# Pooled attention with a gated convolution feed-forward layer: batch 0 loaded as 32-bit words over another queue, some stores moved, last tiles at full height, a new order

## The chip, the cores and the metric

The kernel runs on one core of a Trainium2 chip. Its engines work side by side, each through its own fixed list of instructions: TensorE (PE, matrix products, with weight loads shown as PEld), VectorE (DVE), ScalarE (ACT), GpSimd (POOL) and SyncE (SP). SP and POOL also issue transfers (DMAs); these run on 16 DMA engines that all queues share. The metric is the device time of one execution in microseconds (us), the median of the runs shown; lower is better. A profile is one execution taken by the hardware profiler.

## The reference

There are 8 batches, 8 heads, 576 positions and a head dimension of 64. Keys and values are averaged over groups of 8 positions, which leaves 72 of each per head. The attention output, with the heads side by side (512 columns), goes through a feed-forward layer of 1,024 columns with a gate from a convolution over three positions.

```python
k_p = k.reshape(B, H, Sp, pool, D).mean(axis=3)          # pool = 8, Sp = 72
v_p = v.reshape(B, H, Sp, pool, D).mean(axis=3)
scores = scale * np.matmul(q, k_p.transpose(0, 1, 3, 2))
attn = softmax(scores)                                   # over the 72 pooled keys
x = np.matmul(attn, v_p)                                 # heads put side by side: (8, 576, 512)
h = np.maximum(x @ w_in, 0.0)                            # 512 -> 1024
conv_out[s] = sum over k of conv_w[k] * h[s + k - 1]     # three positions, zero outside
out = (h / (1.0 + np.exp(-conv_out))) @ w_out            # 1024 -> 512
```

Inputs and output are fp32. The products run in bf16 and accumulate in fp32.

## The kernel before

**Stages of a batch.** Each batch passes through the same steps, named as in the code.

- Loads. `load_k` and `load_v` fetch rows of 512 values, one row for each group of 8 positions (8 positions times 64); `load_q` fetches q with 8 consecutive positions on a partition, or, for batches 5 to 7, position by position. All of these, and the weights `w_in` and `w_out`, are issued by GpSimd, which casts fp32 to bf16 on the way. Beside them GpSimd has only a few memsets and masks. In its list a ninth transfer waits for the first of the eight before it.
- Pooling. `pool8` and `attn_k` add the 8 positions of k on DVE in three halving steps (L632, L639, L649). PE transposes the result (L662 for four full tiles of 128 rows, L663 for a last one of 64 rows) and `kz` copies it to a block layout (L669). `attn_v` does the same for v without the transposes, and multiplies by a mask that separates the heads (L700, L705). The mask is made on GpSimd.
- Queries. `regroup` brings the heads of q side by side (L453, on ACT or DVE, for batches 0 to 4). `attn_q` transposes q by PE (L735) and copies it out of PSUM (L744); for batches 5 to 7 it is transposed by DMAs on SP (L718).
- Scores. `attn_s` makes five tiles of products (L767; the fifth by narrow products, L769) and takes the exponential on ACT (L775).
- AV. `attn_av` makes five tiles of 128 positions, the last of 64, with four products (L792) and two more (L796) each. The sums of the weights come out of the same products; DVE takes their reciprocal (L805) and scales (L809) into `xx`. `xx` is transposed to `xT`, for batches 0 to 4 by PE (L829) and a copy (L835), for batches 5 to 7 by DMA transposes on SP (L822).
- Feed-forward. `mm1` (L849 in parts for batch 0, L872 after that) and its relu on ACT; `conv_off` on DVE and ACT (L918 to L945) or `conv_pe` on PE (L995) for a few columns; the gate, its product on DVE (L983); then `mm2` (L1026) for two batches at a time (a pair), a copy to `osb` (L1049, ACT or DVE, three buffers) and a store of up to 512 KB issued by SP (L1054). The last tile of all is done in two halves (L1039, L1044).

**What sets the order.** A planner in the program holds all operations with their dependencies, a written priority for each (`PARAMS["prio"]`) and estimates of their durations. It goes through them in modelled time, and the instructions are emitted in the order that it finds. Each engine then runs its list strictly in that order. `PARAMS["act"]` names the copies, scalings and the like that go to ACT rather than DVE. Where the planner sees a gap on PE in the first 60 us, `warm` fills it with products of a tile of zeros (L407).

**Lines that the change touches.** `load_k`, `load_v`, `load_q` and `regroup` for batch 0; the transposes in `attn_k`; the products in `attn_av` and the last `xx` transpose with its copy; the stores in `mm2`; the priorities and the ACT list. `gT`, two large buffers for the gated activations of a pair, are first written well after batch 0's attention.

Of the kernel before, what the change touches and what calls it, by code (L numbers as in the profile page):

```python
# [17 lines left out]
        "6 14 12 18 16 17 25 33 43 49 53 56 58 61 63 40 38 59 46 54 60 9 32 28 34 31 24 22 "  # L18
        "37 29 20 42 39 27 21 35 41 5 2 3 47 11 8 0 30 4 7 13 44 15 36 19 23 10 1 69 "
        "90 75 80 84 62 182 143 45 52 55 57 64 65 51 48 73 78 70 74 26 66 67 77 50 79 72 89 86 "  # L20
        "85 111 88 83 94 82 87 68 71 76 81 93 91 102 126 124 92 115 97 103 112 101 118 99 96 105 98 114 "
        "100 133 119 107 131 109 116 125 113 136 121 110 146 104 141 148 151 157 132 164 120 108 117 106 129 127 123 128 "
        "95 165 174 179 186 189 167 218 172 178 169 173 185 188 175 181 194 201 203 224 234 202 210 211 219 204 184 208 "
        "207 217 221 213 226 233 241 245 231 236 239 244 249 122 130 142 134 150 158 156 161 160 168 152 137 155 138 154 "
        "176 192 135 140 145 149 139 144 147 162 163 170 153 159 171 180 216 200 265 267 220 230 190 196 205 212 193 197 "
        "232 240 247 255 261 266 183 191 177 187 209 225 199 206 195 229 198 237 253 250 277 260 286 293 316 324 328 338 "
        "349 335 355 348 359 370 215 166 223 228 248 257 262 291 304 317 235 214 242 256 238 243 227 222 246 274 287 303 "
        "312 309 321 345 310 327 344 362 334 351 326 340 365 377 381 393 402 380 385 386 411 413 379 387 389 406 412 398 "
        "399 401 408 415 395 400 404 410 417 252 254 289 299 306 320 264 251 270 278 294 322 318 353 292 263 271 305 330 "
        "297 276 302 308 313 339 341 268 273 275 288 300 307 284 283 290 296 311 315 323 258 269 282 285 331 301 280 298 "  # L30
        "329 347 342 350 336 361 371 382 388 384 392 403 407 428 450 461 476 494 507 272 259 295 314 325 319 337 358 369 "
        "374 352 357 360 368 367 376 363 366 281 333 346 343 364 354 418 423 448 457 391 396 427 419 463 451 459 477 480 "
        "484 491 449 489 483 502 528 485 493 495 525 512 501 503 508 522 530 519 524 532 539 542 442 460 488 498 482 506 "
        "475 505 509 520 533 556 576 583 439 444 437 473 447 446 456 478 455 465 469 474 479 486 504 515 429 435 534 541 "
        "443 440 420 454 453 550 552 514 521 529 537 548 569 546 555 570 579 586 591 578 603 616 638 629 685 696 640 656 "
        "674 708 717 279 332 356 375 373 378 383 422 434 426 397 390 414 425 466 470 467 481 464 416 513 452 538 431 421 "
        "430 433 436 511 517 523 531 540 543 497 500 551 549 559 526 564 604 608 590 596 599 610 624 601 607 620 639 647 "
        "611 623 625 642 646 626 631 637 645 641 547 499 568 575 572 585 600 581 584 614 627 630 636 635 573 580 577 561 "
        "588 594 622 598 609 617 652 644 671 675 605 618 562 571 633 612 628 597 643 650 666 651 665 664 593 606 587 595 "
        "634 654 649 632 658 663 673 677 684 676 699 716 721 724 751 746 761 782 756 767 776 784 802 394 409 438 432 424 "  # L40
        "441 445 471 405 487 554 510 592 544 613 496 589 468 615 545 458 462 472 535 565 707 710 718 679 722 729 709 715 "
        "686 694 738 687 736 768 744 692 749 760 743 704 763 798 754 706 759 777 757 732 788 789 667 683 648 659 690 668 "
        "725 680 705 728 731 735 747 809 661 669 681 688 682 697 698 719 720 733 753 765 774 780 657 662 693 703 727 711 "
        "670 714 726 745 739 758 783 795 734 740 712 702 750 742 755 741 769 775 808 810 814 822 845 860 861 872 874 886 "
        "911 903 912 916 518 582 553 574 492 516 527 557 560 567 558 678 566 700 621 372 619 490 563 713 536 653 655 660 "
        "672 785 790 771 779 766 772 773 762 786 801 793 811 804 815 803 812 819 818 806 817 816 825 841 843 846 851 839 "
        "848 850 856 796 807 813 821 824 829 827 823 834 837 835 844 936 855 832 840 826 830 842 828 849 858 847 862 883 "
        "871 885 890 857 863 820 831 865 833 864 836 873 889 888 884 893 898 853 869 838 852 868 854 867 859 876 881 896 "
        "899 905 891 918 926 941 929 948 950 961 972 966 980 969 977 982 602 689 695 770 764 781 748 730 723 752 737 701 "
        "691 778 792 787 878 879 900 917 791 797 800 805 794 799 925 945 931 935 927 930 934 940 937 947 978 959 946 943 "  # L50
        "953 955 956 968 962 967 880 892 895 902 908 913 897 915 919 924 939 928 949 954 906 920 914 951 922 952 944 965 "
        "960 964 971 974 994 983 870 875 882 887 901 904 907 894 923 910 921 932 938 942 866 877 958 963 909 970 957 933 "
        "973 975 984 979 986 989 1010 1019 1014 1021 1025 1023 1032 1038 1041 1055 1005 1012 1000 1004 1008 1009 1015 1007 1020 1018 1024 1022 "
        "1028 1033 981 991 976 985 1027 1034 988 990 993 995 999 1037 1039 1002 1016 992 1001 1030 1035 1003 1011 1006 1013 1017 1045 1042 "
        "996 998 987 997 1046 1044 1026 1029 1031 1036 1040 1047 1048 1043 1051 1052 1059 1050 1053 1049 1056 1054 1058 1060 1071 1057 1061 1062 "
        "1064 1063 1066 1069 1067 1068 1065 1070 "
# [5 lines left out]
    "act": (  # L62
        "dw1.0 dw1.1 dw4.0 dw5.0 dw6.0 dw6.1 kz.0.0 qg.0.0 qTe.0.0 qTe.0.3 xte.0.2 kz.1.0 "
        "kz.1.1 qg.1.0 qTe.1.0 xte.1.0 xte.1.2 xte.1.4 cp0.0.0 oe.0.0 oe.0.1 oe.0.2 oe.0.3 kz.2.0 "
        "qTe.2.0 qTe.2.1 qTe.2.2 xte.2.0 xte.2.1 xte.2.2 cp2.1.0 cp2.1.4 oe.0.4 oe.0.5 oe.0.6 oe.0.7 "
        "oe.0.8 kz.3.0 qTe.3.0 xte.3.0 xte.3.1 xte.3.2 cp0.2.0 cp0.2.1 cp0.2.3 cp2.2.5 oe.1.0 oe.1.1 "
        "oe.1.2 oe.1.3 kz.4.1 qTe.4.2 xte.4.0 xte.4.1 xte.4.3 cp0.3.0 cp2.3.0 cp2.3.2 cp0.3.4 cp0.3.5 "
        "cp2.3.6 oe.1.5 oe.1.6 oe.1.7 oe.1.8 kz.5.0 kz.5.1 cp2.4.1 cp2.4.3 cp0.4.7 oe.2.2 cp0.5.2 "
# [32 lines left out]
    "qs": [1, 0, 0, 0, 0, 0, 0, 0],  # L101
    "xw": 0,
    "qd": [0, 0, 0, 0, 0, 0, 0, 0],
    "vp": [0, 0, 0, 0, 0, 0, 0, 0],
}


# [201 lines left out]
def kernel(  # L309
# [138 lines left out]
    def regroup(b, pr):  # L448
        if PARAMS["rg"][b] in "QT" or PARAMS["qd"][b]:
            return  # L450
# [707 lines left out]
```

## Time and profile before

| what | us |
|---|---|
| median of three runs | 201.82 (201.66 to 203.79) |
| the profiled run | 200.92 |
| its span, first to last instruction | 199.1 |
| PE busy | 190.8 |
| DVE busy | 171.0 |
| ACT busy | 167.0 |
| POOL busy | 47.5 |
| mm2 products (L1026, psfB) | 65.5 in 282 |
| mm1 products (L872) | 59.2 in 448 |
| products of zeros (L407, both tiles) | 14.9 in 206 |

The granted TensorE clock is 1.000 over the whole run. Busy time of PE counts from the start of a product to its modelled end, and neighbouring products overlap, so a busy PE may still lose time between two starts. In a row of the timeline the first number is the start in us from the beginning of the span, the second the duration; then come the engine, the line, the operation, the tile written and the tiles read, the shapes, and, in brackets, idle time before it and what ended it. "out<-in" names are the program's tiles; psfA, psbB and the like are PSUM tiles. L numbers are lines of the kernel above. In the table of stages each row begins with the stretch, its length, and the busy time of PE, PEld, DVE, ACT and POOL, with the number of instructions in brackets; the last three numbers are the granted clock, the share of the DMA engines and GB/s. Queue q0 carries GpSimd's transfers, q1 those that SP issues.

### The profile page before, as it was taken

The page shows a single profiled execution, that of the slowest core. Times are in us where ns is not written, and L with a number is a line of the kernel's source. Part 1 is how long each engine was busy: PE and PEld are TensorE (multiplying, and loading weights), DVE is VectorE, ACT ScalarE, POOL GpSimd, SP SyncE. Part 2 cuts the span into 40 slices and gives each one's busy share as a digit, 9 for nine tenths or more (in the row PEclk, how much of TensorE's full clock was granted, in tenths as well). Part 3 has the DMA queues.
Part 4 walks back from the last instruction along what each step waited for, and adds up shares of the span by engine and source line. Part 5 has one row for each costly group of instructions (what it writes and reads, how often), then busy time and mean ns, then how long its engine had stood idle before and what let it go on. Part 6 is the DMA issues. An engine that isn't in the chain of part 4 may idle for free.

```text
span 199.1 us, 4491 instructions
## 1 busy us (share of the span) xinstructions
PE 190.8 (96%) x1737; PEld 128.9 (65%) x1737; DVE 171.0 (86%) x400; ACT 167.0 (84%) x282; POOL 47.5 (24%) x76
## 2 busy tenths in 40 slices
PE   5999999999999999999999999989999999999992
PEld 5888777777546576767756656547666565765541
DVE  3777999999999999999999999988889997755631
ACT  0677699999995499999999999995999999998410
POOL 7966431543233262761140000000000000000000
PEclk9999999999999999999999999999999999999999
DMA  3999999999999999999999966477112144502324
GB/s 39 185 185 200 204 204 193 207 206 200 195 204 250 268 217 207 159 217 121 113 116 117 70 211 161 85 189 188 28 35 83 65 129 87 211 3 77 135 106 158
DMA packets 52857, 30.00 MB, mean 151 GB/s; under 512 B 33484, under 2 KB 48356, under 8 KB 52836
## 3 DMA queue, kind: packets, MB, share of 16 engines
q0 software_dynamic: 32912, 16.73, 68.1%
q1 hardware_dynamic: 19924, 12.99, 26.9%
q8 instruction: 13, 0.21, 0.4%
q14 instruction: 8, 0.07, 0.1%
HBM read 33.44 MB, written 9.44 MB: 215 GB/s over the span
## 4 chain that ended last, share of the span: by engine, by line
PE 88%; DVE 7%; POOL 2%; DMA 1%; issue 1%; ACT 0%; POOLq 0%
PE psfB L1026 31%; PE psfA L872 25%; PE psfA L792 4%; PE psfA L767 4%; PE psfA L995 4%; PE pswA L407 3%; PE psbB L735 2%; PE psfB L849 2%; DVE xx L809 2%; PE psfA L849 2%; PE psfA L796 2%; PE psbB L829 1%; PE pswB L407 1%; PE psbA L829 1%; DMA xT<-xx 1%; PE psfA L769 1%
## 5 line engine op out<-in xcount | busy, mean ns | idle before, releaser
L1026 PE MATMUL psfB<-w_out,gT 128*128 128x512 bf16 (+1 forms) x282 | 65.5, 378 | 0.0
L872 PE MATMUL psfA<-xT,w_in 128*128 128x288 bf16 x448 | 59.2, 286 | 0.9 <-DMA xT<-xx 0.7
L872 PEld LDWEIGHTS <-w_in 128*128 128x128 bf16 x448 | 42.8, 98 | 14.8 <-issue 1.2
L1026 PEld LDWEIGHTS <-gT 128*128 128x128 bf16 x290 | 27.2, 98 | 29.0 <-issue 0.2
L878 ACT ACTIVATE hT<-psfA 128x576 bf16<-128x576 f32 x56 | 35.2, 651 | 2.2 <-PE psfA L872 2.0
L918 ACT ACTIVATE cv<-hT,cr 128x576 bf16<-128x576 bf16 x37 | 28.3, 779 | 0.2
L809 DVE TENSOR_TENSOR xx<-psfA,rr 128x512 bf16<-128x512 f32 (+1 forms) x40 | 26.8, 683 | 0.9 <-DMA xT<-xx 0.7
L920 DVE TENSOR_SCALAR cv<-hT,cr 128x576 bf16<-128x576 bf16 x71 | 23.9, 363 | 3.9 <-ACT tg L945 2.3
L775 ACT ACTIVATE attnT<-psfA 128x576 bf16<-128x576 f32 x40 | 25.1, 674 | 0.3 <-PE psfA L767 0.2
L983 DVE TENSOR_TENSOR gT<-tg,hT 128x1152 bf16<-128x1152 bf16 x32 | 23.7, 750 | 1.2 <-ACT tg L1002 0.8
L927 DVE TENSOR_TENSOR cv<-cv,hT 128x1152 bf16<-128x1152 bf16 (+1 forms) x31 | 20.8, 672 | 4.0 <-ACT cv L918 3.9
L945 ACT ACTIVATE tg<-cv,cn 128x576 bf16<-128x576 bf16 x31 | 23.2, 775 | 0.9 <-DVE cv L937 0.6
L937 DVE TENSOR_TENSOR cv<-cv 128x1152 bf16<-128x1152 bf16 (+1 forms) x31 | 20.8, 673 | 0.2
L1049 ACT COPY osb<-psfB 128x512 f32<-128x512 f32 x24 | 14.3, 595 | 7.4 <-PE psfB L1026 7.3
L945 ACT ACTIVATE tg<-cv,cs 128x576 bf16<-128x576 bf16 x23 | 17.5, 797 | 0.0
L792 PE MATMUL psfA<-vblk,attnT 128*128 128x130 bf16 (+1 forms) x160 | 15.7, 222 | 0.2
L407 PEld LDWEIGHTS <-zero 128*128 128x128 bf16 x206 | 13.0, 105 | 3.4 <-DVE zero L520 2.5
L792 PEld LDWEIGHTS <-attnT 128*128 128x128 bf16 (+1 forms) x160 | 11.0, 100 | 4.1 <-issue 1.8
L407 PE MATMUL pswA<-zero 128*128 128x128 bf16 x148 | 10.5, 236 | 2.5 <-DVE zero L520 2.5
L767 PE MATMUL psfA<-qT,kz 128*128 128x512 bf16 x64 | 12.3, 286 | 0.4 <-ACT attnT L775 0.4
L439 POOL DMA_DIRECT2D q<-in_q_dram x10 | 8.6, 863 | 12.1 <-DMA k_b<-in_k_dram 4.0
L796 PE MATMUL psfA<-vblk,attnT 128*128 128x130 bf16 (+1 forms) x80 | 11.2, 221 | 0.0
(94 smaller groups left out, 247.8 us busy)
## 6 DMA issues: line engine op xcount, KB each, us to landing
out_dram<-osb SPq DMA_DIRECT2D x14, 512.0 KB, 3.0
k_b<-in_k_dram POOLq DMA_DIRECT2D x8, 512.0 KB, 14.8
v_b<-in_v_dram POOLq DMA_DIRECT2D x7, 512.0 KB, 16.7
q_b<-in_q_dram POOLq DMA_DIRECT2D x4, 576.0 KB, 17.6
out_dram<-osb SPq DMA_DIRECT2D x7, 256.0 KB, 2.1
w_in<-in_moe_w_in_dram POOLq DMA_DIRECT2D x2, 512.0 KB, 11.4
w_out<-in_moe_w_out_dram POOLq DMA_DIRECT2D x2, 512.0 KB, 15.0
q<-in_q_dram POOLq DMA_DIRECT2D x8, 128.0 KB, 12.6
```

Source lines behind the costliest of these rows:

```text
L407: nc.tensor.matmul(out=t, lhsT=zero[:, 0:P], rhs=zero[:, 0:P], start=True, stop=True)
L775: nc.scalar.activation(out=attnT[m][:, t, :], in_=slot(key).rearrange("p i x -> p (i x)")[:, 0:S], func=ACT.Exp, scale=1.0 / 64.0)
L792: nc.tensor.matmul(out=a[0:n, g, c * w:(c + 2) * w], lhsT=attnT[m][:, s, u0:u0 + n], rhs=vblk[m][:, 2 * s:2 * s + 2, :].rearrange("p x d - ...
L809: nc.vector.tensor_tensor(out=xx[i3][0:n].rearrange("p (g h e) -> p g h e", g=2, h=4), in0=av_view()[:, :, :, 0:D], in1=rr[i3][0:n].rearra ...
L872: nc.tensor.matmul(out=t[:, i, 0:HC], lhsT=w_in[:, c, f * P:(f + 1) * P], rhs=xT[m][:, c, i * HC:(i + 1) * HC], start=(c == 0), stop=(c == ...
L878: nc.scalar.activation(out=h_(b)[:, f, hs(b), 2:S + 2].rearrange("p (i x) -> p i x", i=2), in_=slot(key)[:, :, 0:HC], func=ACT.Relu)
L918: nc.scalar.activation(out=cv[y][:, kk // 2, z0:z1, :], in_=src, func=ACT.Copy, scale=sc)
L920: nc.vector.tensor_scalar(out=cv[y][:, kk // 2, z0:z1, :], in0=src, scalar1=sc, scalar2=None, op0=OP.mult)
L927: nc.vector.tensor_tensor(out=cv[y][:, 0, 0:n, :], in0=cv[y][:, 0, 0:n, :], in1=h_at(2), op=OP.add)
L945: nc.scalar.activation(out=tg[i3][:, zs[z0]:zs[z0] + z1 - z0, :], in_=cv[y][:, 0, z0:z1, :], func=ACT.Tanh if half else ACT.Sigmoid, scale ...
L983: nc.vector.tensor_tensor(out=o_, in0=tg[i3], in1=h2, op=OP.mult)
L1026: nc.tensor.matmul(out=a[:, 0, j0:j1], lhsT=g[:, c, t * P:(t + 1) * P], rhs=w_out[:, c, j0:j1], start=(c == 0), stop=(c == n_fb - 1), skip ...
```

## The change

- Batch 0's q, k and v are issued by SP instead of GpSimd. Nothing is cast: they land as fp32 words in the two `gT` buffers, which are idle then (`ks`, `ws`, `qs`). The first adds of k and v and the regroup of q read fp32. The regroup of batch 0 becomes four pieces of two heads, all on ACT. q comes first in SP's list (heads 4 to 7), then the convolution weights, k, the rest of q, and v.
- GpSimd's list therefore begins with memsets, the identity and then the loads of batch 1 and `w_in`.
- The stores of pairs 1 and 2 go to GpSimd's queue (ten stores), after all of its loads. Pairs 0 and 3 stay on SP.
- The last transpose of k takes 128 rows (64 of them zeros) instead of 64. The last tile of AV takes 128 columns of weights; the 64 beyond the end are the next tile's columns or a pad of zeros, and their results are not used. The last tile of `xx` goes through ordinary products with 128 rows into fp32 PSUM instead of 64-row transposes into bf16.
- Four memsets are added on DVE (the unwritten parts of the fp32 tiles, the two pads).
- The priorities and the ACT list are all new, and some estimates in the planner change, so that every engine's order differs. In the new lists PE has 146 products of zeros instead of 206. After batch 0, ACT has 5 scalings of the convolution fewer (32 of 108 instead of 37), 3 output copies more (27 instead of 24) and all five copies of `xx`'s last tiles; DVE the reverse.

```diff
@@ PARAMS
-    "prio": (...), "act": (...)
+    "prio": (...), "act": (...)
+    "kh": 2,
+    "sp": [0, 1, 1, 0],
...
-    perm4 = st("perm4", [64, 64], BF16)
+    perm4 = st("perm4", [P, 64], BF16)
...
-    attnT = [st(f"attnT{i}", [P, NT, S], BF16) for i in range(2)]
+    attnF = [st(f"attnT{i}", [P, NT * S + 64], BF16) for i in range(2)]
+    attnT = [a[:, 0:NT * S].rearrange("p (t s) -> p t s", t=NT) for a in attnF]
...
@@ load_q
+        if b == 0 and PARAMS["kh"] == 2:
+            for x in range(2):
+                for y, (r0, r1) in enumerate(((0, 64), (64, PR))):
+                    def fn(e, x=x, r0=r0, r1=r1):
+                        nc.sync.dma_start(out=qs[x][r0:r1].rearrange("p h i d -> p h (i d)"), in_=rows_q(b)[r0:r1, 4 * x:4 * x + 4])
...
@@ regroup
+        if b == 0 and PARAMS["kh"] == 2:
+            for h in range(0, H, 2):
+                def fn(e, h=h):
+                    copy_on(e)(out=q2[0][0:PR, :, h:h + 2, :], in_=qs[h // 4][0:PR, h % 4:h % 4 + 2].rearrange("p h i d -> p i h d"))
...
+    def early(i, lo, hi):
+        return gT[i].rearrange("p f s -> p (f s)")[:, lo:hi].bitcast(FP32)
+    ks = early(1, 0, NT * 1024).rearrange("p (t e) -> p t e", t=NT)
+    ws = early(0, 0, NT * 1024).rearrange("p (t e) -> p t e", t=NT)
+    qs = [early(i, NT * 1024, NT * 1024 + 4096).rearrange("p (h i d) -> p h i d", i=TP, d=D) for i in range(2)]
...
@@ load_k
+        if b == 0 and PARAMS["kh"]:
+            def fn(e):
+                nc.sync.dma_start(out=ks[:, 0:4], in_=src[0:512].rearrange("(t p) e -> p t e", p=P))
...
+                nc.sync.dma_start(out=ks[0:64, 4], in_=src[512:576])
...
@@ load_v
+        if b == 0 and PARAMS["kh"] == 2:
+            for c in range(4):
+                def fn(e, c=c):
+                    nc.sync.dma_start(out=ws[32 * c + 16:32 * c + 32, 4], in_=src[P:P + 16, c])
...
+            for x in range(2):
+                def fn(e, x=x):
+                    nc.sync.dma_start(out=ws[:, 2 * x:2 * x + 2], in_=src[0:P, 2 * x:2 * x + 2])
...
@@ attn_k
-            nc.tensor.transpose(out=t[:, 0, 512:576], in_=ksum[0:64, 4].rearrange("p i d -> p (i d)"), identity=ident[0:64, 0:64])
+            nc.tensor.transpose(out=t[:, 0, 512:640], in_=ksum[:, 4].rearrange("p i d -> p (i d)"), identity=ident)
...
@@ attn_av
-                nc.tensor.matmul(out=a[0:n, g, c * w:(c + 2) * w], lhsT=attnT[m][:, s, u0:u0 + n],
+                nc.tensor.matmul(out=a[:, g, c * w:(c + 2) * w], lhsT=attnF[m][:, s * S + u0:s * S + u0 + P],
...
-                nc.tensor.matmul(out=a[0:n, g, 0:4 * w].rearrange("p (c x d) -> p c x d", x=2, d=w)[:, :, 1], lhsT=attnT[m][:, 4, u0:u0 + n],
+                nc.tensor.matmul(out=a[:, g, 0:4 * w].rearrange("p (c x d) -> p c x d", x=2, d=w)[:, :, 1], lhsT=attnF[m][:, 4 * S + u0:4 * S + u0 + P],
...
-            a = slot(key2, True)
+            a = slot(key2, not last)
             for c in range(n_dc):
-                nc.tensor.transpose(out=a[:, 0, c * P:c * P + n], in_=xx[i3][0:n, c * P:(c + 1) * P], identity=(ident[0:n, 0:n] if tr else perm4 if last else perm))
+                if last:
+                    nc.tensor.matmul(out=a[:, 0, c * n:(c + 1) * n], lhsT=xx[i3][:, c * P:(c + 1) * P], rhs=ident[:, 0:n] if tr else perm4, start=c == 0, stop=c == n_dc - 1, skip_group_check=True)
+                    continue
+                nc.tensor.transpose(out=a[:, 0, c * P:c * P + n], in_=xx[i3][0:n, c * P:(c + 1) * P], identity=(ident if tr else perm))
...
@@ mm2
-            nc.sync.dma_start(out=out_rows[r:r + n * P, :].rearrange("(i p) d -> p i d", p=P), in_=osb[i3][:, 0:n, :])
+            (nc.gpsimd if PARAMS["sp"][pair] else nc.sync).dma_start(out=out_rows[r:r + n * P, :].rearrange("(i p) d -> p i d", p=P), in_=osb[i3][:, 0:n, :])
```

## The prediction

> **What bounds the kernel now.** I read the page's shares and its chain of waits first, then busy time by stage, then the timeline of the start, then the places where PE changes its tile, and last the DMA queues.
>
> ```profile
> PE 190.8 (96%) x1737; PEld 128.9 (65%) x1737; DVE 171.0 (86%) x400; ACT 167.0 (84%) x282; POOL 47.5 (24%) x76
> ...
> PE 88%; DVE 7%; POOL 2%; DMA 1%; issue 1%; ACT 0%; POOLq 0%
> ```
>
> PE carries 88% of the chain that ended last. The stages (columns: length, PE, PEld, DVE, ACT, POOL) show that it is not alone:
>
> ```profile
> 31.00:130.00 99.00, 98.80 (x895) 65.97 (x892) 97.18 (x225) 93.00 (x161) 28.10 (x36) 1.00 1.35 175
> 130.00:136.00 6.00, 4.65 (x52) 2.70 (x51) 5.07 (x14) 4.59 (x8) 0.00 (x0) 1.00 0.69 197
> ```
>
> From 31 to 130 us PE and DVE are both full (98.80 and 97.18 of 99 us), so time taken off PE alone is not all won. From 130 to 136 PE has a hole. The start is a chain of transfers (start, duration, engine, what):
>
> ```profile
> 8.45 0.82 DVE L632 TENSOR_TENSOR p<-k_b 128x1280 bf16<-128x1280 bf16 x1 [0.28 <-DMA k_b<-in_k_dram]
> 11.41 0.69 DVE L453 COPY q<-q_b 72x2048 bf16<-72x2048 bf16 x1 [0.33 <-DMA q_b<-in_q_dram]
> 14.79 0.56 DVE L632 TENSOR_TENSOR p<-v_b 128x768 bf16<-128x768 bf16 x1 [0.32 <-DMA v_b<-in_v_dram]
> 15.90 1.35 PE L407 MATMUL pswB<-zero 128*128 128x128 bf16 x21
> 17.09 0.40 PE L792 MATMUL psfA<-vblk,attnT 128*128 128x130 bf16 x4
> ```
>
> k is in at 8.45, q at 11.41, all of v at 14.79, and PE fills time with products of zeros until AV starts at 17.09.
>
> **Full tile height.** The first three rows are a last AV tile (64 columns of weights) and the product after it, the next two an ordinary AV tile, then k's transposes and what follows:
>
> ```profile
> 102.40 0.42 PE L792 MATMUL psfA<-vblk,attnT 128*64 128x130 bf16 x4
> 102.66 0.28 PE L796 MATMUL psfA<-vblk,attnT 128*64 128x130 bf16 x2
> 102.87 0.39 PE L1026 MATMUL psfB<-w_out,gT 128*128 128x512 bf16 x1
> ...
> 121.75 0.40 PE L792 MATMUL psfA<-vblk,attnT 128*128 128x130 bf16 x4
> 122.11 0.40 PE L792 MATMUL psfA<-vblk,attnT 128*128 128x130 bf16 x4
> ...
> 126.86 0.39 PE L662 MATMUL psbB<-ident,ksum 128*128 128x128 bf16 x4
> 127.31 0.66 PE L767 MATMUL psfA<-qT,kz 128*128 128x512 bf16 x4
> ```
>
> Starts count here, since ends overlap. A narrow AV tile holds PE from 102.40 to 102.87, 0.47 us; the product before it should have passed the array on at 102.31 (eight at 0.216 us from 100.58), so 0.09 more is lost going in. A full one holds it 0.36 (121.75 to 122.11). Gain 0.21 us; 7 of the 8 stand among real work (batch 0's does not): 1.5 us. k's five transposes hold it 0.45; at full height they are five like those of x, twelve of which take 0.67 in the chain, 0.056 each, 0.28. Gain 0.17 for batches 2 to 7 (0 and 1 are followed by zeros): 1.0 us. x's last tile (88.94 to 89.16, and 0.10 going in) costs 0.32; four products of 64 columns should pass like the 72-column ones of q (ten in 0.33 in the chain), 0.13. Gain 0.19 for batches 1 to 4: 0.8. Sum 3.3 us of PE.
>
> The Trainium skill, "TensorEngine Tiling (Array Packing)", section Theoretical Speedup, speaks against this edit: a dimension of at most 64 may run up to 2x faster in a small tile. By it the six narrow products would take half of 0.36 us, and making them full would cost 0.18 us seven times, 1.3 us, in place of the 1.5 won. The trace disagrees: four narrow products start 0.26 us after one another (102.40 to 102.66), four full ones 0.24 (121.75 to 121.99). That page's Key Properties say that a change of tiling mode drains the array, as the 0.09 us do.
>
> Will DVE and ACT let it through? Counted in the two orders, after batch 0, DVE gains 5 conv scalings (0.36 each) and a kz copy (0.31), loses 3 output copies (0.69), 4 x ends (0.28; all five go to ACT, now from fp32 PSUM) and 2 qT copies (0.53): -2.2 us. ACT loses 5 scalings (0.78) and a kz copy (0.39), gains 3 output copies (0.60), 4 x ends (0.39) and 2 qT copies (0.80): +0.8, with 6 us idle in the long stage. DVE's relief is below PE's 2.9 before 130 us; two narrow AV tiles (0.4) come later. I take -2.8; ends -0.4 (only those two) and -3.3.
>
> **Batch 0 as 32-bit words.** q, k and v are 576 rows of 2 KB each, 1,728 packets on SyncE's queue. A 512 KB store of 256 such packets shows the rate: alone 248 packets in 149.1 to 150.4 us, 190 a us; beside GpSimd's loads (60.1 to 62.1):
>
> ```profile
> q1 hardware_dynamic: 200, 0.41, 57.8%
> q0 software_dynamic: 266, 0.18, 55.8%
> ```
>
> 100 a us. A store issued at 56.33 behind a GpSimd backlog had its first packet at 60.04. SP issues from 0.81 us, 0.43 apart, first packets 1.0 us after issue (the cw_raw load): alone, k is in at about 7.5, q at 9.4, v at 12.5. But GpSimd, freed of batch 0, now starts batch 1's q at about 1.9 us; its first bulk ran 2.8 us after issue (k's, issued 2.16, full rate by 5.0). If that backlog waits behind SP's as the store did (3.7 us), the queues share from 8.4 and the last 680 packets need 7.1 us: v at 15.9. Reads on SP's queue beside loads are nowhere in this trace.
>
> What follows the data also grows. DVE's fp32 adds: by the 128x512 fp32 copies (0.69) 1.3 ns a column, so 0.95 and 0.65 us for v's pieces instead of 0.56 and 0.41, both now behind the last piece: 2.9 us to AV, against 2.3. ACT takes the whole q regroup, four of 0.95 (1.90 for 2048 columns); fp32 costs it nothing extra (fp32 and bf16 copies of 512 columns, 0.595 and 0.594). Its queue: conv weights in at about 5.0 (the load is now fourth on SP's queue), table 1.28, six scalings of 0.31, four regroups, one copy 0.63: 12.6. Then transposes 0.3, DVE copy 0.46, scores 0.4, five exps in 2.9: AV not before 16.7. So AV starts at 16.7 if SP's queue keeps ahead, 18.8 if it shares: -0.4 to +1.7 against 17.09. I take +0.8, leaning to the one row that shows a late comer waiting.
>
> GpSimd's early start pays in batch 1: 27 products of zeros (chain: 0.66, 0.78 and a bit) wait there around 27 to 30 us, after k at 24.5. Now k of batch 1 is in after 1,728 + 576 + 512 + 640 packets, at 190 a us about 21. I take -1.0 of 1.5; ends 0 and -1.5. Masks go behind eight loads on POOL (0.54 to 0.88 each), to about 9.5 us, hidden by the k add; if not, everything behind them on DVE waits. Four more memsets on DVE (the largest about 0.54, twice the 0.27 of 256 words) lie before any data.
>
> **Stores of pairs 1 and 2 on GpSimd's queue.**
>
> ```profile
> 130.64 0.53 SPq L1054 DMA_DIRECT2D out_dram<-osb  x1
> 131.26 2.68 SPq L822 DMA_TRANSPOSE xT<-xx  x2
> ```
>
> The transpose of x tile 3, batch 5, could follow the one that ended issuing at 130.55; it waits for the store's wait and issue to 131.26, tile 4 follows, and PE's products wait for them until 135.09. With only transposes queued, 0.7 us go directly, and more by the order. PE is idle 1.35 us in this stage and loses 3.0 by gaps between starts. I take -1.0; ends 0 and -3.0. On POOL the ten stores follow all loads (done at 108 us; the first such store ran at 114.19), so nothing queues behind them; three output buffers cover a slower landing, and without that cover one tile's 1.73 us waits.
>
> **New order.** Rewritten on every engine. PE loses about 4.5 us by gaps from 31 to 130 us; a different order can lose 2 more or less. I take 0.
>
> **Sum.** -2.8 + 0.8 - 1.0 - 1.0 = -4.0. Span 199.1 to 195.1, the profiled run 200.92 to 196.9; the median of the three runs is 0.9 higher (201.82), so 197.8.
>
> **Rivals.** (1) All comes through: SP's queue keeps its lead, DVE yields, the hole at 130 closes: -0.4 - 1.5 - 3.3 - 3.0 = -8.2, 193.6. For it: every piece has a row. Against: DVE's 98%.
> (2) Slower: GpSimd's loads interleave with batch 0 as soon as they flow, at 4.7 us. Some 440 packets are then through; the other 1,290 at 95 a us end at 18.3, AV starts at 21.6, 4.5 us late. DVE, which sets the pace to 130 us with its queue in fixed order, starts its full stretch that much later and eats the gain on PE but for 0.4: 201.8 + 4.5 - 0.4 - 1.0 = 204.9. It decides from a delay of 1.4 us on (over 1% from 3.4). For it: the equal shares at 60.1. Against: the 3.7 us before them. The Trainium skill, "DMA: Bandwidth & Descriptors", Rules for kernel authors, states it: spreading DMAs over issuing engines brings no bandwidth, they interleave. By that the time is this rival's; the shares agree.
> (3) Swallowed: SP nearly keeps up, but DVE holds PE and new gaps take the hole's place: +0.8 - 0.4 - 1.0 + 0.5 = -0.1, 201.7.
> That the edit is not made is excluded: the changed order has no narrow AV, k or x products and twelve batch-0 loads on SP.
>
> **Numbers.** Forecast 0.48 (195.8 to 199.8), rivals 0.22, 0.17, 0.13. About 1% is what a measurement here tells from no change: 199.8 to 203.8. Faster 0.22 + 0.46 = 0.68; same 0.13 + 0.02 = 0.15; slower 0.17. The range reaches from rival 1 to near rival 2: 193.6 to 203.6.
>
> **What would show it.** The first AV product near 17.9 us; v's add at 12.5 (SP ahead), 16 or 18.7 (interleaved); no zeros after the first AV tiles; AV's last tile 0.35 us long and k's transposes 0.28, with no 0.09 going in; fewer than 1 us of PE idle around batch 5's x; DVE below 98% in the long stage. Wrong if PE's idle or zeros grow by what the tiles save, or if DVE's adds of v start after 18 us.

## The result and the profile after

The changed kernel is slower: 210.45 us median of four runs (209.2 to 211.76) beside 202.12 (201.66 to 203.79) for the kernel before, measured beside it, a ratio of 1.0398 (95% interval 1.0307 to 1.0489). The forecast was 197.8, at most 203.6. The profiled run took 210.9 us with a span of 209.1. Ratios, here and below, leave out executions more than 1.5% above the fastest of the same kernel.

The first rows of the page, its row of the granted clock and the chain of waits answer to those of before:

```profile
PE 188.6 (90%) x1677; PEld 129.2 (62%) x1677; DVE 170.1 (81%) x400; ACT 169.1 (81%) x288; POOL 48.5 (23%) x76
...
PEclk9999997999999999999999999999999999999999
...
PE 52%; DVE 22%; DMA 11%; ACT 9%; issue 2%; SPq 1%; ACTq 0%; DVEq 0%
```

PE does 2.2 us less than before, yet carries only 52% of the chain instead of 88%; DMA, 1% before, has 11%. The place is the start. The timeline (start, duration, engine, line, what):

```profile
7.48 8.35 SPq L520 DMA_DIRECT2D gT<-in_v_dram  x3
...
8.31 0.30 PE L593 MATMUL psfB<-identf,cw_raw 24*128 24x24 f32 x1 [4.08 <-DMA cw_raw<-in_moe_conv_w_dram]
...
16.46 1.49 DVE L693 TENSOR_TENSOR p<-gT 128x1280 bf16<-128x1280 f32 x1 [3.12 <-DMA gT<-in_k_dram]
...
19.63 1.99 ACT L469 CAST q<-gT 72x1024 bf16<-72x1024 f32 x2 [4.35 <-DMA gT<-in_q_dram]
...
26.65 1.56 DVE L693 TENSOR_TENSOR p<-gT 128x768 bf16<-128x768 f32 x2 [3.97 <-DMA gT<-in_v_dram]
...
29.77 0.40 PE L861 MATMUL psfA<-vblk,attnT 128*128 128x130 bf16 x4 [3.67 <-DVE vblk L769]
```

The add of k starts at 16.46 us (8.45 before), that of v at 26.65 (14.79), each after a wait for its transfer, and AV at 29.77 instead of 17.09: 12.7 us late. The two transfers on the chain that ended last are k's, and the last of v's small pieces, which SP could issue only after it (start, duration):

```profile
2.98 12.53 DMA gT<-in_k_dram
15.53 10.91 DMA gT<-in_v_dram
```

The span is only 10.0 us longer, so what follows the first AV product is 2.7 us shorter, 179.3 instead of 182.0. The stages (columns as in the table of before):

```profile
31.00:130.00 99.00, 96.02 (x933) 67.72 (x931) 96.58 (x226) 91.44 (x163) 34.12 (x43) 0.98 1.24 168
130.00:136.00 6.00, 6.00 (x52) 3.89 (x50) 6.00 (x14) 5.98 (x11) 0.57 (x1) 1.00 0.50 114
```

The hole at 130 us is gone (PE 6.00 of 6.00 instead of 4.65). DVE is below 98% from 31 to 130, but PE is now idle for 3 us there.

The edits on PE came out as read. k's transposes, an AV tile and the last tile of x, each with the product behind it:

```profile
62.79 0.39 PE L727 MATMUL psbB<-ident,ksum 128*128 128x128 bf16 x4
63.01 0.22 PE L728 MATMUL psbB<-ident,ksum 128*128 128x128 bf16 x1
63.07 2.40 PE L1067 MATMUL psfA<-hT,dw 128*128 128x288 bf16 x18
...
83.45 0.40 PE L861 MATMUL psfA<-vblk,attnT 128*128 128x130 bf16 x4
83.69 0.28 PE L865 MATMUL psfA<-vblk,attnT 128*128 128x130 bf16 x2
83.81 1.89 PE L1098 MATMUL psfB<-w_out,gT 128*128 128x512 bf16 x8
85.53 0.28 PE L899 MATMUL psfB<-perm,xx 128*128 128x64 bf16 x4
85.65 0.61 PE L901 MATMUL psbA<-perm,xx 128*128 128x128 bf16 x8
```

By starts: 0.28 us for k, 0.36 for an AV tile, 0.12 for x, with no narrow tile and no 0.09 us of change left.

What the queues did shows in the packets from 9 to 13 us (queue, packets, MB, share of the 16 engines):

```profile
q0 software_dynamic: 384, 0.38, 56.3%
q1 hardware_dynamic: 379, 0.76, 55.7%
```

Batch 0 on q1 and batch 1 with `w_in` on q0 take turns here, 95 packets a us each. Before that it was no equal share: from 6 to 8 us GpSimd's queue had 457 packets through and SP's 90.

### The profile page after: what moved, and what is told of

It is laid out like the page before. It is cut to its first block, busy times and chain, and to the rows that moved or that the text cites. A ratio compares the mean times of both kernels' runs of the same rounds, so it can differ in the third digit from the quotient of the medians.

```text
span 209.1 us, 4391 instructions
## 1 busy us (share of the span) xinstructions
PE 188.6 (90%) x1677; PEld 129.2 (62%) x1677; DVE 170.1 (81%) x400; ACT 169.1 (81%) x288; POOL 48.5 (23%) x76
## 4 chain that ended last, share of the span: by engine, by line
PE 52%; DVE 22%; DMA 11%; ACT 9%; issue 2%; SPq 1%; ACTq 0%; DVEq 0%
PE psfB L1098 21%; PE psfA L944 19%; DMA gT<-in_k_dram 6%; DMA gT<-in_v_dram 5%; DVE p L693 4%; PE psfA L861 3%; DVE cv L992 3%; DVE xx L878 2%; DVE cv L1009 2%; DVE p L701 2%; DVE cv L999 2%; PE psfA L1098 2%; ACT tg L1017 2%; ACT hT L928 1%; PE psfA L1067 1%
## 5 line engine op out<-in xcount | busy, mean ns | idle before, releaser
L1098 PE MATMUL psfB<-w_out,gT 128*128 128x512 bf16 (+1 forms) x274 | 63.5, 377 | 0.1
L992 DVE TENSOR_SCALAR cv<-hT,cr 128x576 bf16<-128x576 bf16 x76 | 26.5, 372 | 2.3 <-ACT hT L928 0.9
L1017 ACT ACTIVATE tg<-cv,cn 128x576 bf16<-128x576 bf16 x32 | 24.6, 792 | 1.5 <-DVE cv L1009 1.5
L990 ACT ACTIVATE cv<-hT,cr 128x576 bf16<-128x576 bf16 x32 | 24.8, 793 | 0.2
L1121 ACT COPY osb<-psfB 128x512 f32<-128x512 f32 x26 | 15.1, 596 | 8.2 <-PE psfB L1098 7.9
L1126 POOL DMA_DIRECT2D out_dram<-osb x10 | 6.9, 686 | 63.4 <-ACT osb L1121 39.7
L861 PE MATMUL psfA<-vblk,attnT 128*128 128x130 bf16 x160 | 15.8, 223 | 4.2 <-DVE vblk L769 3.7
L861 PEld LDWEIGHTS <-attnT 128*128 128x128 bf16 x160 | 11.8, 100 | 8.3 <-issue 4.2
L415 PEld LDWEIGHTS <-zero 128*128 128x128 bf16 x146 | 11.8, 123 | 4.0 <-DVE zero L568 3.5
L447 POOL DMA_DIRECT2D q<-in_q_dram x10 | 9.5, 949 | 9.0 <-DMA v_b<-in_v_dram 4.4
```

Source lines behind the costliest of these rows:

```text
L861: nc.tensor.matmul(out=a[:, g, c * w:(c + 2) * w], lhsT=attnF[m][:, s * S + u0:s * S + u0 + P], rhs=vblk[m][:, 2 * s:2 * s + 2, :].rearran ...
L990: nc.scalar.activation(out=cv[y][:, kk // 2, z0:z1, :], in_=src, func=ACT.Copy, scale=sc)
L992: nc.vector.tensor_scalar(out=cv[y][:, kk // 2, z0:z1, :], in0=src, scalar1=sc, scalar2=None, op0=OP.mult)
L1017: nc.scalar.activation(out=tg[i3][:, zs[z0]:zs[z0] + z1 - z0, :], in_=cv[y][:, 0, z0:z1, :], func=ACT.Tanh if half else ACT.Sigmoid, scale ...
L1098: nc.tensor.matmul(out=a[:, 0, j0:j1], lhsT=g[:, c, t * P:(t + 1) * P], rhs=w_out[:, c, j0:j1], start=(c == 0), stop=(c == n_fb - 1), skip ...
```

## The experiments

All times are beside runs of the kernel before on the same chip. The table gives, from the profiled execution of each, the start of the first AV product, the span, and what lies between that product and the end, which is nearly the same work in every kernel (the height of the tiles differs, and how much of batches 0 and 1 falls ahead of it). It is one execution each, and that of before, 200.92 us, is faster than its median, so differences of a microsecond in these columns prove little. The last column is the ratio of the times, over all runs, with its interval.

| kernel | first AV | span | after it | ratio |
|---|---|---|---|---|
| before | 17.09 | 199.1 | 182.0 | 1 |
| changed | 29.77 | 209.1 | 179.3 | 1.0398 (1.0307 to 1.0489) |
| e1 before, full height | 18.11 | 199.9 | 181.8 | 0.9937 (0.99 to 0.9974) |
| e4 before, stores moved | 17.94 | 200.4 | 182.5 | 1.0034 (0.9994 to 1.0073) |
| e2 changed, GpSimd held for v | 20.57 | 205.1 | 184.5 | 1.0174 (1.0099 to 1.025) |
| e3 changed, GpSimd held for k | 21.74 | 200.3 | 178.6 | 1.0006 (0.9965 to 1.0046) |
| e7 e3, k in halves | 23.86 | 204.7 | 180.8 | one run, 206.52 us |
| e8 changed, loads back on GpSimd | 24.03 | 203.5 | 179.5 | 1.0112 (1.0077 to 1.0148) |
| e9 e8, k on SP | 23.92 | 202.5 | 178.6 | 1.0105 (1.0073 to 1.0138) |
| e10 changed, only q on SP | 20.72 | 199.2 | 178.5 | 0.9983 (0.994 to 1.0026) |
| e11 e8, regroup divided | 19.81 | 198.7 | 178.9 | 0.9938 (0.9906 to 0.9969) |
| e12 start in order of arrival | 21.50 | 199.6 | 178.1 | 0.9957 (0.9928 to 0.9985) |
| e13 e12 with narrow tiles | 21.01 | 201.5 | 180.5 | 1.0046 (1.0012 to 1.0081) |
| e14 scores in pairs | 20.13 | 198.5 | 178.4 | 0.9942 (0.9912 to 0.9973) |
| e15 e14 without zeros between | | | | 0.9922 (0.9889 to 0.9955) |

**Full height alone, in the old order.**

```diff
# before.py; likewise k's last transpose and the last tile of xx
-    out=a[0:n, g, c * w:(c + 2) * w], lhsT=attnT[m][:, s, u0:u0 + n],
+    out=a[:, g, c * w:(c + 2) * w], lhsT=attnF[m][:, s * S + u0:s * S + u0 + P],
```

> The kernel before with the full-height ends of k, AV and x alone, in its old order. Theory (PE sets the pace, DVE lets most through): last AV tile 0.36 us on PE instead of 0.47 and no 0.09 going in, k's transposes 0.28 instead of 0.45; 2.0 to 3.3 us less, about 199.3. Rival (DVE, 98% busy from 31 to 130 us, holds PE): less than 0.7 us, about 201.6, with new gaps on PE where the tiles shrank.

It gained 0.63%, 1.3 us (0.5 to 2.0), between the two. The profiled execution doesn't show this gain (its span is 0.8 us longer, with a start 1.0 us later), but its stages say where time stayed; the row from 60 to 100 us is from e1, with that of before under it:

```profile
31.00:130.00 99.00, 96.93 (x895) 65.82 (x888) 96.42 (x224) 91.82 (x160) 29.90 (x37) 1.00 1.39 176
130.00:136.00 6.00, 4.76 (x52) 2.60 (x50) 5.26 (x14) 5.79 (x11) 0.00 (x0) 1.00 0.64 164
```

```profile
60.00:100.00 40.00, 39.42 (x416) 28.62 (x415) 39.81 (x95) 34.81 (x61) 16.60 (x20) 1.00 1.50 194
60.00:100.00 40.00, 39.83 (x412) 28.11 (x409) 39.16 (x95) 34.47 (x61) 16.13 (x21) 1.00 1.51 193
```

For the same 895 products from 31 to 130 us PE is busy 1.87 us less than before (98.80), but the stretch holds no more of them: the time became idle time on PE. Up to 100 us DVE is full (39.81 of 40 us), so it holds the pace there. After that DVE itself waits for a load; the first add of one batch's k, in e1 and in before:

```profile
113.29 0.83 DVE L634 TENSOR_TENSOR p<-k_b 128x1280 bf16<-128x1280 bf16 x1 [2.19 <-DMA k_b<-in_k_dram]
111.78 0.82 DVE L632 TENSOR_TENSOR p<-k_b 128x1280 bf16<-128x1280 bf16 x1 [0.32 <-DMA k_b<-in_k_dram]
```

So a second thing stood behind PE here, the arrival of k on GpSimd's queue, which the prediction has nowhere among its limits of this stage. How much of the gain it kept back is not known; it is one execution.

**Stores of pairs 1 and 2 alone, in the old order.**

```diff
# before.py
-            nc.sync.dma_start(out=out_rows[r:r + n * P, :]...
+            (nc.gpsimd if pair in (1, 2) else nc.sync).dma_start(out=out_rows[r:r + n * P, :]...
```

> The kernel before with the stores of pairs 1 and 2 on GpSimd's queue alone, old order. Theory (the transposes of batch 5's x wait behind a store on SP): the transposes that were issued at 131.26 go out 0.5 to 0.8 us earlier, the product after them starts at about 134 instead of 135.1, total 0.7 to 1 us less, about 201.2. Rival (the hole comes from the order, xx itself is late): within 0.3 us of before, 202.

No gain: the interval runs from 0.12 us less to 1.5 more, and the rival's "within 0.3 us" lies in it. The hole stays (PE busy 4.38 of 6 us, 4.65 before):

```profile
130.00:136.00 6.00, 4.38 (x50) 2.56 (x49) 4.51 (x12) 5.02 (x9) 0.72 (x1) 1.00 0.81 189
```

So the store between two transposes on SP did not make it. In the changed kernel it went with the new order, stores moved; tall tiles are not needed for that (e13, with narrow ones, has PE busy 5.95 of the 6 us), and the order without the moved stores wasn't tried.

**GpSimd's loads held back.** A small copy on GpSimd, ahead of its first load, reads what SP loads, so that load waits; the masks are moved ahead of it.

```diff
# after.py
+            if o.name == "ldq1.0":                     # GpSimd's first load
+                nc.gpsimd.tensor_copy(out=held, in_=ws[:, 0:4, 0:1])   # e2: v's two large pieces
+                nc.gpsimd.tensor_copy(out=held, in_=ks[:, 0:4, 0:1])   # e3 instead: k's large piece
```

> The changed kernel, but GpSimd's first load (batch 1's q) follows a small copy that reads both large pieces of batch 0's v, so that no GpSimd load runs beside batch 0; the masks come before it. Theory (the loads of GpSimd halve SP's queue): k's first add at 8 to 10 us instead of 16.5, v's at 13 to 15 instead of 26.7, first AV product at 17 to 18.5 instead of 29.8, and the total 8 to 11 us under 210.4, less what batch 1 and w_in then come late. Rival (SP's queue reads fp32 slowly by itself): v's add after 18 us, AV after 21.

> The same, but GpSimd's loads wait only for k's large piece. Theory: k's add at 8 to 10 us as in the run that holds for v; the 832 packets behind it share from there on: v's add at 17 to 19, first AV product at 20 to 22, and the total between that run and the changed kernel, or below both if batch 1's loads matter more. Rival (SP slow by itself): k's add at 12 or later.

With v awaited (e2), v's add starts at 17.23 and AV at 20.57: 9.2 us of the 12.7 are gone, so GpSimd's loads beside batch 0's cost that much. AV lies between the 17 to 18.5 of the theory and the "after 21" of its rival. But batch 1's q then comes too late: PE waits 2.9 us for its copy and runs at half clock from 24 to 31 us, and the rest is 184.5. With k awaited (e3) GpSimd's packets begin at 15 us, and the time is that of before (1.0006): AV is still 4.65 us late, and 3.4 us come back behind it. k was in at 10.9 us, where the expectation had 7.5:

```profile
12.04 1.48 DVE L694 TENSOR_TENSOR p<-gT 128x1280 bf16<-128x1280 f32 x1
...
18.63 1.56 DVE L694 TENSOR_TENSOR p<-gT 128x768 bf16<-128x768 f32 x2 [1.25 <-DMA gT<-in_v_dram]
...
21.74 0.40 PE L862 MATMUL psfA<-vblk,attnT 128*128 128x130 bf16 x4 [0.95 <-DVE vblk L770]
```

Still, even with SP's queue alone, v's large pieces (in at 16.4 us, when GpSimd's held copy ran in e2) are far from the 12.5 of the forecast. In e3 the queue carries k between 7 and 9 us, q's second piece between 9.8 and 12 (packets, MB, rate of the stretch):

```profile
DMA packets 376, 0.76 MB, mean 382 GB/s; under 512 B 3, under 2 KB 3, under 8 KB 376
```

```profile
DMA packets 219, 0.44 MB, mean 198 GB/s; under 512 B 6, under 2 KB 6, under 8 KB 219
```

q goes at half of k's rate. q's pieces fill 64 partitions, k's 128.

**k cut into two pieces of 64 partitions**, on e3.

```diff
# e3
-                nc.sync.dma_start(out=ks[:, 0:4], in_=...
+                for p0 in (0, 64):
+                    nc.sync.dma_start(out=ks[p0:p0 + 64, 0:4], in_=...[p0:p0 + 64])
```

> The kernel that holds GpSimd's loads until k's large piece is in, with that piece (128 partitions) cut in two of 64 partitions each, one behind the other on SyncE's queue. There q's two pieces of 64 partitions went at 198 GB/s (9.8 to 12 us), k's of 128 at 382 (7 to 9 us). Theory (the number of partitions sets it): k's pieces go at about 200 GB/s, k's add comes at 14 to 15 instead of 12.04 us, v's at 21 instead of 18.63, first AV near 24, span near 203. Rival (it is how q lies in memory, or the first touch of a tensor): k's pieces at 350 to 390 GB/s, add at 12 to 12.5, AV at 21 to 22.5, span 199.5 to 201.5.

From 7 to 9 us, where k went at 382 GB/s:

```profile
DMA packets 210, 0.40 MB, mean 199 GB/s; under 512 B 16, under 2 KB 16, under 8 KB 210
```

The same words from the same rows of memory now go at half the rate, v's add moves from 18.63 to 20.75 us and AV to 23.86, as expected; k's own add came earlier than the 14 to 15 expected, at 12.90. It is one run. Rows, words and queue are the same, so it is the number of partitions. The Trainium skill, "SBUF — State Buffer", section "Door 1: The DMA port swizzle (why `[64,N]` ≈ `[32,N]`)", states it: partitions 0 to 63 reach only 8 of the 16 ports, with 196 GB/s measured for 64 partitions and 328 for 128. These runs agree on 64 partitions, with 198 and 199, and on the halving; their 382 for 128 is above the page's 328.

**Batch 0 back on GpSimd's queue, all else as changed.** In e5 and e6 batch 2's load of q stood ahead of half of batch 0's regroup, which therefore waited for it and read batch 2's q for four heads: the two kernels (e5 with all on GpSimd, 1.1071, 1.1007 to 1.1136; e6 with k on SP, 1.0963, 1.0896 to 1.103) say nothing on the question.

> The changed kernel with batch 0's q, k and v back on GpSimd's queue as bf16, issued before batch 1's; every engine's other work in the changed kernel's order, stores and full tile height kept. Theory (the loss is all in batch 0's loads; behind the first AV product the changed kernel was 2.7 us shorter, 179.3 instead of 182.0 us, by the tiles and the order): first AV between 17 and 18.5 us as before, span near 197, time 198 to 199.5, ratio 0.975 to 0.987. Rival A (the shorter body came from batch 1's loads, which ran while PE waited for batch 0): AV at 17 to 18.5, products of zeros back around 25 to 30 us, body 181 to 182, span 199 to 200, ratio 0.99 to 1.00. Rival B (the new order itself costs): ratio over 1.01.

> As the run before, but k of batch 0 on SyncE's queue as 32-bit words, with nothing but the convolution weights ahead of it; q and v on GpSimd's queue. Theory (two queues share one rate of some 180 packets a us, so it matters only that what shares with batch 0 is batch 0 itself; the second queue starts earlier): k's add at 9 to 11 us, q's regroup at 9.5 to 11, v's add at 13.5 to 14.5, first AV at 16 to 17.5, 0.5 to 1.5 us before that of the run with all on GpSimd's queue, time as much less. Rival (sharing delays k and q each to the end of both): k's add at 11.5 or later, first AV at 18 or later, time 0.5 to 1.5 us more than that run's.

With that load behind the regroup (e8, e9):

```diff
# after.py; e9 leaves k's load as it is and moves DVE's adds of k ahead of its first copy of transposed q
-                nc.sync.dma_start(out=ks[:, 0:4], in_=...
+                nc.gpsimd.dma_start(out=k_b[0][:, 0:4], in_=...        # v and q likewise
+        plan.insert(plan.index(by["qg.0.0"]) + 1, by["ldq2.0"])
```

> Batch 0's q, k and v on GpSimd's queue again, the rest as in the changed kernel, with batch 2's load of q now behind all four pieces of batch 0's regroup (in the first attempt it stood ahead of two of them). Theory (the loss is all in batch 0's loads; behind the first AV product the changed kernel is 2.7 us shorter, 179.3 instead of 182.0 us, by the tiles and the order): first AV between 17 and 18.5 us, span near 197, time 198 to 199.5, ratio 0.975 to 0.987. Rival A (the shorter body came from batch 1's loads, which ran while PE waited for batch 0): AV at 17 to 18.5, zeros back around 25 to 30 us, span 199 to 200, ratio 0.99 to 1.00. Rival B (the new order itself costs): ratio over 1.01.

> As the run before, but k of batch 0 on SyncE's queue as 32-bit words behind the convolution weights, and DVE's adds of k ahead of its first copy of transposed q. In the first attempt k's packets went at 157 to 189 a us from 3 to 5 us and were through by 7.3, q's by about 9.5. Theory: k's add at 8 to 8.5 us, q's regroup at 10.5 to 11, v's add at 13.5 to 14.2, first AV at 16 to 17, 0.5 to 1.5 us ahead of the run with all on GpSimd's queue, time as much less. Rival (something else ends last before AV, ACT's four pieces of the regroup and the exponentials behind them): AV within 0.4 us of that run's, same time.

Both missed the start that was expected, with AV at 24 us, and are 1.1% slower than before. (e8's ratio is its rival B's, over 1.01, but the loss lies ahead of AV and not behind it.) The timeline of e8:

```profile
11.14 1.99 ACT L470 COPY q<-q_b 72x1024 bf16<-72x1024 bf16 x2 [1.71 <-DMA q_b<-in_q_dram]
...
14.47 4.53 PE L415 MATMUL pswA<-zero 128*128 128x128 bf16 x54
...
15.23 1.99 ACT L470 COPY q<-q_b 72x1024 bf16<-72x1024 bf16 x2
...
20.69 0.88 DVE L694 TENSOR_TENSOR p<-v_b 128x768 bf16<-128x768 bf16 x2
```

Data is not late here: nothing in the last three rows waits for a transfer. The four pieces of the regroup are all on ACT, the second pair behind scalings and a copy, and 54 products of zeros, set for a q that comes early, hold PE until 19 us. So the new order has a start that was laid out for other arrival times. In e9 k's add came at 8.80 us, near the 8 to 8.5 expected, and nothing came of it, as the rival had it: v's add at 20.57, AV at 23.92. But behind AV both have 178.6 to 179.5 us, like the changed kernel.

**Only q on SP.**

```diff
# after.py: q as changed, k and v on GpSimd ahead of batch 1; in the order:
+        for n in ("qT.0.1", "av.0.0"):
+            pl.gaps[by[n][3].i] = (0.6, *pl.gaps[by[n][3].i][1:])    # shorter blocks of zeros
```

> The changed kernel with q of batch 0 on SyncE's queue as now, but its k and v on GpSimd's queue as bf16, ahead of batch 1's loads; two blocks of products of zeros ahead of the first AV product cut to 0.6 us each. Theory (what hurts is batch 1's loads beside batch 0's, and q's pieces of 64 partitions passing at half the rate of k's; with q alone on one queue its slowness is covered by k and v on the other, and what follows the first AV product takes 178.6 to 179.5 us as in the runs with the changed order): q's first regroup at 7 to 8 us, k's add at 9 to 10, v's add at 13 to 14.5, first AV at 16 to 17.5, span 195 to 197, time 197 to 199, ratio 0.973 to 0.985. Rival A (start as good, but what follows grows by what the start saves, since batch 1's loads come later): span 199 to 200, ratio 0.99 to 1.00. Rival B (two queues start each other late, v's add after 16): AV after 18.5, ratio above 0.99.

A miss at the start, as its rival B had it: q's regroup began at 12.03 us, not 7 to 8, k's add at 13.96, not 9 to 10, v's at 18.28 and AV at 20.72. From 4 to 12 us q on SP and k on GpSimd took turns (187 packets to 217 from 6 to 8). The time is that of before.

**The start mended, loads on GpSimd.**

```diff
# e8
+        block = [(x, "DVE", z, o) if o.name in ("qg.0.6", "qg.0.4") else (x, y, z, o) ...]   # behind k's adds
+        # blocks of zeros as in e10; loads of batch 0 in the order of before
```

> The changed kernel with all of batch 0's loads on GpSimd's queue in the order of the kernel before, heads 4 to 7 of q regrouped on DVE behind k's adds (ACT does the other four), and the two blocks of zeros cut to 0.6 us each: the two things that held the first AV product to 24 us in the last two runs. Theory: first AV at 17 to 18.5 us, 178.6 to 179.5 us behind it, span 196 to 198, time 197.5 to 199.5, ratio 0.976 to 0.988. Rival (what follows grows to the 182 us of the kernel before once the start is as early): span 199 to 200.5, ratio 0.99 to 1.00.

```profile
17.37 0.88 DVE L694 TENSOR_TENSOR p<-v_b 128x768 bf16<-128x768 bf16 x2
...
19.81 0.28 PE L862 MATMUL psfA<-vblk,attnT 128*128 128x130 bf16 x2
```

It beats both kernels, 0.9938, with 178.9 us behind AV as the theory had it, but AV is 2.7 us later than in the kernel before (v's add stands behind copies of q on DVE), not at 17 to 18.5, so the expected ratio of 0.976 to 0.988 was missed. Four more kernels went for an earlier start and a division of the gain:

```diff
# e12, against e11: k's transposes ahead of q, no zeros between the transposes; both copies of k and qTe.0.1 to 0.3 on DVE
+        block = [... "kT.0 kz.0.0 kz.0.1 qg.0.6 qg.0.4 qg.0.2 qg.0.0 ldq2.0 qT.0.3 qTe.0.3 qT.0.2 ..."]
# e13: e12 with the narrow tiles of before
# e14: all four copies of transposed q on DVE, 30 and 13 zeros ahead of k's and q's transposes, first scores ahead of the last transpose
# e15: e14 without the zeros between q's transposes, fewer ahead of AV, the mask's conversion later
```

> The run before (all loads of batch 0 on GpSimd's queue), with the rest of the start in order of arrival: k's transposes and copies ahead of q, three of the four copies of transposed q on DVE, ACT's two pieces of the regroup back to back, and no products of zeros between them. Theory (what follows the first AV product takes 178.6 to 179.5 us in the changed order at full tile height, whatever the start): first AV at 17 to 18 us, span 196 to 197.3, time 197.5 to 199.3, ratio 0.973 to 0.985. Rival (the gain of 2.7 us behind the first AV product is there only while the start is late, since batch 1's loads and DVE have caught up by then): first AV at 17 to 18, span 198.5 to 200, ratio 0.985 to 1.00.

> The same with the last tiles of k, AV and x narrow again, as in the kernel before; order, loads and stores unchanged. Theory (full height is worth as much as it gave alone in the old order, 0.6%, some 1.2 us; the order gives the rest): 1 to 1.6 us more than the kernel beside it. Rival A (DVE set the pace in the old order and hid part of it; in the new order all 3.3 us of PE come through): 2.5 to 3.5 us more. Rival B (the order gives it all): within 0.5 us of it.

> All loads of batch 0 on GpSimd's queue, order behind the start as changed, full tile height. In the last two runs PE ran at half rate in the start (six score products took 1.64 instead of 0.91 us), since the zeros between its steps were gone, and scores waited for all of q. Here zeros fill PE up to q again (30 before k's transposes, 13 before q's), all four copies of transposed q are on DVE, and the first scores and their exponential stand ahead of the last transpose. Theory (what follows the first AV product takes 178 to 179.5 us, whatever the start): first AV at 17.2 to 18.5 us, span 195.5 to 198, time 197 to 199.5, ratio 0.97 to 0.985. Rival (the 2.7 us are lost again when the start is as early as before): first AV at 17.2 to 18.5 us, span 199 to 200.5, ratio 0.985 to 1.00.

> As the run before, without the three zeros that stood between its transposes of q (they wrote the PSUM bank of the first scores and so waited for their exponential until 16.69 us), with the mask's conversion behind k's sums, and with 3 zeros instead of 12 ahead of the first AV product. Theory (178 to 179.5 us behind the first AV product): first AV at 17.8 to 18.8 us, span 196 to 198, time 198 to 199.8, ratio 0.976 to 0.988. Rival (the gain shrinks as the start comes nearer to 17.1): span 198.3 to 200, ratio 0.99 to 1.00.

None of e12, e13 and e14 reached AV at 17 or 18 us, and the ratios of e12, e14 and e15 lie where their rivals had them (0.985 or 0.99 to 1.00). In e12 PE ran at half rate for a while: six products of scores took

```profile
16.64 1.64 PE L837 MATMUL psfA<-qT,kz 128*128 128x512 bf16 x6
```

where e11 shows

```profile
17.02 0.91 PE L837 MATMUL psfA<-qT,kz 128*128 128x512 bf16 x6
```

The row of the granted clock shows 9 throughout in both, so it doesn't show this stretch. Fewer products of zeros, and so more idle PE ahead of it, are the likely reason; that is not shown, as e11 had a longer single wait there (2.25 us against 1.88).

In e14 three zeros wrote the bank of the first scores and waited for their exponential:

```profile
16.69 0.33 PE L415 MATMUL pswA<-zero 128*128 128x128 bf16 x3 [0.74 <-ACT attnT L845]
```

e15 took them out and came to 0.9922; its profiled execution had the clock at half from 12.9 to 30 us, so its start is not read here. e13 against e12 gives the worth of full height in the new order: 0.9% (1.0046 to 0.9957), 1.8 us with 0.9 to either side, more than the 1 to 1.6 expected and less than rival A's 2.5 to 3.5, though the interval reaches both.

## Why the prediction was wrong

**The step that failed** is the one on the two queues: "If that backlog waits behind SP's as the store did (3.7 us), the queues share from 8.4 and the last 680 packets need 7.1 us: v at 15.9", and with it AV at 17.9 (+0.8). Measured: v's add at 26.65, AV at 29.77 (+12.7). The runs put three things in its place:

- GpSimd's queue did not wait behind SP's. Its packets began between 5 and 6 us, from 6 to 8 us it had 457 through to SP's 90, and from 8 us the queues took turns, as they did at 60.1 us in the trace of before. The store that waited 3.7 us there was SP's own, behind a flow of GpSimd's; the prediction turned this round. What those 3.7 us were no run shows. Holding GpSimd until v is in gives back 9.2 us.
- SP's queue was slow by itself: 190 packets a us were read from a store of 128 partitions, but q's two large pieces, 512 of batch 0's 1,728 packets, go to 64 partitions and pass at half of that. Cutting k the same way, 512 packets again, moved v's add and AV by 2.1 us. The start was also slower than 190: 239 packets of 2 KB were through at 5 us, not the 600 that this rate gives from 1.8 us.
- v's small tails were issued late: SP's row of three issues at 7.48 us lasts 8.35 us, 5.0 of them a wait for k. The last tail, issued at 15.53, landed at 26.4 and is on the chain that ended last; v's add follows at 26.65. But the tail issued at 7.48 took 18.3 us and landed at 25.8, so the late issue by itself puts v only some 0.6 us back. This wait was not in the forecast; it wasn't tried alone.

Rival 2 had the mechanism, a chance of 0.17 and 204.9 us; the range ended at 203.6, short of it. Its size was off too, 4.5 us late instead of 12.7: it took 440 packets as through when sharing began and 95 a us after that; in fact 320 were through by 6 us, and 74 a us followed up to 25 us, tails included.

The Trainium skill's rule quoted there ("DMA: Bandwidth & Descriptors", Rules for kernel authors: issuing engines interleave) is borne out by the 384 and 379 packets, though from 6 to 8 us the shares were far from equal.

**Full tile height, -2.8.** The 3.3 us on PE are there, row by row. The time is -1.3 in the old order and -1.8 in the new: the term was mis-sized at the point where the sum let nearly all of it through DVE, on a count of moved operations, while the row of DVE (97.18 of 99) said that it would hold. In e1 PE's idle time shows that the time was not passed on; what stood in the way was DVE up to 100 us and a load of k after that. In the new order with an earlier start DVE is busy 98.1 to 98.4 of the 99 us from 31 to 130 (e3, e10 to e12, e14), so PE's work can hardly be passed on faster there. (The list of moved operations was also added up with 0.1 us of error, to -2.2 for DVE in place of -2.1 and +0.8 for ACT in place of +0.7, which changes nothing.)

**Batch 1's zeros, -1.0.** All but four products of zeros are gone after the first AV product (38 before), but PE had been idle for longer ahead of it. It is a part of the 2.7 us and wasn't measured alone.

**Stores, -1.0.** Wrong: no gain alone, 1.0034 (0.9994 to 1.0073). The hole has another cause. It is gone in the changed kernel and in e13, which share the new order and the moved stores; which change of the order does it wasn't tried.

**New order, 0.** Better than taken behind AV: with narrow tiles the rest is 180.5 us (e13) against 182.0, one execution each, stores and earlier loads included. Worse at the start, where it cost e8 7 us with data that came on time; that cost was not a term of the sum at all.

So what follows the first AV product is 2.5 to 3.9 us shorter in eight of the ten profiled executions with full-height tiles in the new order (e7 1.2, e2 longer by 2.5; e15's, at half clock from 12.9 to 30 us, is left out), of the 4.8 that the forecast gave without the start; the start took 12.7. That the gain would stay with AV at 17 us is not shown: the earliest start tried had 19.8, with 3.1 us of it.

## What to carry to other kernels

A load that is moved to another queue does not only start earlier: it frees its old queue, and what comes forward there shares the engines with it as soon as its packets flow (5.6 us here); hold that work back by a dependency, or leave the urgent load where it was. Read a queue's rate from rows of the same shape, the number of partitions first. And an order that was planned around arrival times is part of those loads: undoing the loads alone (e8) was better than the change, 1.0112 to 1.0398, and still slower than the kernel before.

## What the runs showed of the hardware

- A transfer into 64 partitions went at 198 and 199 GB/s on SP's queue, one into 128 at 382, with packets of 2 KB in both.
- Where PE stood idle for 3.67 us (the changed kernel before 29.77), its clock went to half 1.1 us after it resumed, for 3.4 us (30.9 to 34.3), the 7 in the row of the clock. In e2 half clock lasted 6.8 us after 2.92 us of idleness, in e7 it came from 24.2 to 27.6 us after only 2.10, and in e3 0.95 us had none. The Trainium skill, "TensorE: Matmul & The Clock Gate", section "Part 1: The HAM clock gate", has a window of 3.4 us for this. The length of the two shorter stretches, 3.4 us, agrees; the 2.10 us that preceded one in e7 are less than one window. This suggests that the products of zeros in the start earn their place, as long as they end before data arrives (e8) and use no bank that is in use (e14); no run takes them out alone.
